# Windowed attention with sinks, then a gated MLP block: one load queue with casts on chip, transposes one phase earlier, gating bias on the tensor engine, a shared ring of four PSUM banks

## The chip, the cores and the metric

The kernel runs on one core of one Trainium2 chip. The metric is the device time of a whole execution in microseconds (us). Every kernel was run several times; "before" and the kernel compared with it ran on the same chip, in alternating rounds. Ratios use fast runs alone: a ratio is the mean time of one kernel's fast runs over that of the other's fast runs of the same rounds, so it isn't quite the ratio of the medians quoted beside it.

Names of engines in the profile: PE is the tensor engine (PEld its weight loads), DVE the vector engine, ACT the scalar engine, POOL the GpSimd engine, SP the engine that issues the loads and stores (SPq is its queue).

## The reference, cut to what matters

```python
# q, k, v: (4 batches, 8 heads, 768 positions, 64); n_sink = 4, window = 128
scores = (q @ k.T) / sqrt(64)
keep   = (pos_k < n_sink) | ((pos_q - pos_k >= 0) & (pos_q - pos_k < window))
x      = softmax(where(keep, scores, -1e9)) @ v          # -> (4, 768, 512)
h      = gelu_tanh(x @ w_in)                             # w_in: 512 x 1024
u, vv  = h[..., :512], h[..., 512:]
vn     = layer_norm(vv) * g_ln                           # over the 512 features
vs     = einsum('ts,bsd->btd', w_sg, vn) + b_sg[:, None] # mixes positions, 768 x 768
out    = x + (u * vs) @ w_out                            # f32, (4, 768, 512)
```

## The kernel before

Per batch the kernel has an attention part and an MLP part, and it weaves the attention of batch b+1 into the spatial mixing of batch b. The unit names below recur: T (cast and transpose q and k of a head pair), SK (scores against the sinks), QK, AV, XT (attention), MV (gate half of w_in, gelu, layer norm: the profile's hv, vt, z), MU (other half: hu, uT), SP (spatial mixing: vs, gatedT), OUT (ops, ot).

```python
ps_sc = tile_pool(name="ps_sc", bufs=2, space=PSUM)   # 2 tiles of 2 banks: sc, hv, hu
ps_av = tile_pool(name="ps_av", bufs=2, space=PSUM)   # attention results
ps_mm = tile_pool(name="ps_mm", bufs=2, space=PSUM)   # transposes, scs, vs, ops
...
def load_sinks(b):                                    # eight loads of 4 x 64 for each batch
    t = small.tile([n_sink * H, Dh], F32, name="vs32")
    for h in range(H):
        nc.sync.dma_start(out=t[n_sink * h:n_sink * (h + 1), :], in_=v[b, h, 0:n_sink, :])
...
def T(b, p):
    ...
    pcast(cb, src)                                    # q and k to bf16, both on POOL
    ps = ps_mm.tile([128, NT, 128], BF16, name="trp", tag="mm")
    for t in range(NT):
        nc.tensor.transpose(ps[:, t, :], cb[:, t, :, :], iden)
    # copy out of PSUM: q on DVE (qT), k on ACT (kT); then 2 small DVE copies into ks_sink
...
def QK(b, p, g):
    ...
    nc.scalar.activation(out=pt, in_=sc, func=Exp, scale=scale)
    nc.vector.tensor_mul(pt, pt, m)                   # band mask, every group on DVE
...
def MV(b, jj):
    ...
    nc.gpsimd.tensor_tensor(rs, rs, neg_half[:, 0:2], op=ALU.pow)
    for jl in range(2):                               # z = (vt - mean) * rs
        nc.vector.tensor_scalar(out=z[b][:, 2 * jj + jl, :], in0=vt[:, jl, :],
                                scalar1=mv[:, jl, 0:1], scalar2=rs[:, jl:jl + 1],
                                op0=ALU.subtract, op1=ALU.mult)
...
def SP(b, hf, dc):                                    # 6 products, then DVE, then POOL
    ...
    nc.vector.scalar_tensor_tensor(out=tmp, in0=ps[:, 0:NH], scalar=g_sb[:, dc:dc + 1],
                                   in1=b_bc[:, NH * hf:NH * (hf + 1)], op0=ALU.mult, op1=ALU.add)
    nc.gpsimd.tensor_mul(gatedT[b, hf][:, dc, :], tmp, uT[b][:, dc, NH * hf:NH * (hf + 1)])
...
# weights: three casting loads from the GpSimd queue, f32 in memory to bf16 on chip
nc.gpsimd.dma_start(out=w_in_sb, in_=moe_w_in.rearrange("(c p) f -> p c f", p=128))
...
for b in range(B):
    # MV and MU of batch b, with T(b+1, p) and load(b+2, p) between them;
    # then SP and OUT of batch b woven with SK, QK, AV, XT of batch b+1
```

The softmax here doesn't subtract the row's maximum and nothing guards it: scores larger than these inputs give would overflow.

## Time and profile before

The four runs of the kernel before had a median of 224.09 us (220.84 to 227.33). Two of them (224.35 and 227.33) lie over 1.5% above the fastest and count as slow. The profiled one took 222.34 us, of which 220.6 is the span.

I cut the span into stages. M of a batch starts at the first hv product that the others follow without a break; S starts at the first mixing product after the last z of the batch (a few products of rows already normalized come earlier). What stands ahead of M0 is the prologue: loads and the attention of batch 0.

| | prologue | M0 | S0 | M1 | S1 | M2 | S2 | M3 | S3 | tail |
|---|---|---|---|---|---|---|---|---|---|---|
| starts at, us | 0 | 36.5 | 68.3 | 95.1 | 116.2 | 142.9 | 160.7 | 187.1 | 201.5 | 217.3 |
| length, us | 36.5 | 31.8 | 26.8 | 21.1 | 26.7 | 17.8 | 26.4 | 14.4 | 15.8 | 3.3 |

Two windows of steady S stages are added here, for the comparison later. The columns are the stretch, its length, busy time of PE, PEld, DVE, ACT and POOL with the number of instructions, the granted PE clock, the DMA share and GB/s.

```profile
120.00:130.00 10.00, 7.75 (x93) 4.31 (x93) 9.08 (x15) 5.37 (x6) 4.49 (x4) 1.00 0.14 51
160.00:170.00 10.00, 8.02 (x69) 3.71 (x71) 7.72 (x12) 6.66 (x8) 4.77 (x4) 1.00 0.01 2
```

PE has gaps of some 2 us in 10, and DVE is the fuller engine in the first of the two.

### The profile page before, as it was taken

What the parts mean: (1) busy time and instruction counts of PE and PEld (TensorE: products, weight loads), DVE (VectorE), ACT (ScalarE), POOL (GpSimd) and SP (SyncE); (2) the same over time, 40 slices, a digit from 0 to 9 for tenths busy, and PEclk for the clock granted to TensorE, in tenths of its full rate; (3) what the DMA queues carried; (4) which work ended last, traced back from release to release, by engine and by line L of the source; (5) the groups of instructions that cost most, each with busy time, mean ns of one, the idle gap of its engine ahead of it and who ended that gap; (6) DMA issues with size and microseconds to landing.
All of it is one profiled execution on the core that took longest, in us unless ns stands there. A gap on an engine that the chain in (4) does not pass through costs nothing.

```text
span 220.6 us, 3819 instructions
## 1 busy us (share of the span) xinstructions
PE 165.1 (75%) x1444; PEld 92.8 (42%) x1460; DVE 152.3 (69%) x302; ACT 105.9 (48%) x123; POOL 97.2 (44%) x134
## 2 busy tenths in 40 slices
PE   0653767693959698699649599898796998798792
PEld 0331544351635465445424355545433555344340
DVE  3542788254897898737986898648968986276553
ACT  2250697532644455164758264375792643642000
POOL 8715822466662726506865506026144061034360
PEclk9999999889699999999999999999999999999999
DMA  6986999999994039299800040210000302100213
GB/s 197 266 155 185 279 230 221 306 287 314 289 312 115 0 113 248 54 269 250 211 8 0 0 146 1 95 51 0 0 3 0 143 3 95 48 4 0 76 68 143
DMA packets 39778, 28.59 MB, mean 130 GB/s; under 512 B 26576, under 2 KB 36048, under 8 KB 39760
## 3 DMA queue, kind: packets, MB, share of 16 engines
q1 hardware_dynamic: 37920, 25.60, 41.9%
q0 software_dynamic: 1840, 2.75, 6.9%
q8 instruction: 11, 0.18, 0.4%
q14 instruction: 7, 0.06, 0.1%
HBM read 24.81 MB, written 6.29 MB: 141 GB/s over the span
## 4 chain that ended last, share of the span: by engine, by line
DVE 33%; DMA 18%; PE 18%; POOL 11%; issue 7%; SPq 6%; ACT 4%; POOLq 1%; DVEq 0%; ACTq 0%
DVE z L271 8%; DVE pt L206 7%; PE ops L307 6%; POOL gatedT L301 6%; DMA v_104<-in_v_dram 6%; DMA b_bc<-in_moe_b_sg_dram 5%; DVE gtmp L298 4%; PE vs L294 4%; DVE st L265 3%; ACT pt L204 3%; DVE ot L310 3%; DVE qT L168 3%; POOL rs L269 3%; DMA v_544<-in_v_dram 3%; PE hv L254 3%
## 5 line engine op out<-in xcount | busy, mean ns | idle before, releaser
L301 POOL TENSOR_TENSOR gatedT<-gtmp,uT 128x384 bf16<-128x384 bf16 x32 | 33.9, 1066 | 50.9 <-DVE gtmp L298 50.5
L204 ACT ACTIVATE pt<-sc 128x1024 bf16<-128x1024 f32 (+1 forms) x48 | 43.9, 953 | 22.6 <-PE sc L199 22.4
L294 PE MATMUL vs<-wsgT,z 128*128 128x384 bf16 x192 | 36.6, 327 | 2.3 <-DVE z L271 1.1
L307 PE MATMUL ops<-w_out_sb,gatedT 128*128 128x512 bf16 x89 | 25.6, 381 | 12.0 <-POOL gatedT L301 10.6
L254 PE MATMUL hv<-w_in_sb,xT 128*128 128x512 bf16 x92 | 24.2, 397 | 3.8 <-ACT vt L260 2.1
L168 DVE COPY qT<-trp 128x768 bf16<-128x768 bf16 x16 | 15.2, 951 | 15.8 <-PE trp L164 15.7
L206 DVE TENSOR_TENSOR pt<-pt,mask_128 128x1024 bf16<-128x1024 bf16 (+1 forms) x32 | 25.0, 792 | 1.4 <-ACT pt L204 1.1
L244 ACT COPY xT<-xps 128x768 bf16<-128x768 bf16 x16 | 12.8, 803 | 26.1 <-PE xps L243 26.1
L281 PE MATMUL hu<-xT,w_in_sb 128*128 128x384 bf16 x128 | 24.5, 336 | 0.7 <-ACT uT L284 0.7
L298 DVE SCALAR_TENSOR_TENSOR gtmp<-vs,g_sb,b_bc 128x384 bf16<-128x384 f32 x32 | 19.5, 611 | 7.9 <-PE vs L294 7.9
L310 DVE TENSOR_TENSOR ot<-ops,x_sb 128x512 f32<-128x512 f32 x24 | 16.4, 690 | 11.2 <-PE ops L307 11.2
L294 PEld LDWEIGHTS <-z 128*128 128x128 bf16 x192 | 17.2, 97 | 16.4 <-issue 4.6
L271 DVE TENSOR_SCALAR z<-vt,mv,rs 128x512 bf16<-128x512 f32 x24 | 17.5, 768 | 8.2 <-POOL rs L269 8.2
L199 PE MATMUL sc<-qT,kT 64*128 64x256 bf16 x192 | 19.6, 280 | 2.3 <-DVE rcp L234 1.1
L219 PEld LDWEIGHTS <-pt 128*128 128x128 bf16 x192 | 15.0, 99 | 13.0 <-issue 6.5
L284 ACT ACTIVATE uT<-hu 128x768 bf16<-128x768 f32 x16 | 13.0, 814 | 12.4 <-PE hu L281 12.4
L265 DVE BATCH_NORM_STATS2 st<-vt 128x6 f32<-128x512 f32 x24 | 15.6, 673 | 4.2 <-ACT vt L260 4.2
L170 ACT COPY kT<-trp 128x768 bf16<-128x768 bf16 x16 | 12.8, 801 | 11.3 <-PE trp L164 11.3
L235 DVE TENSOR_TENSOR x_sb<-av,rcp 128x384 bf16<-128x384 f32 x32 | 17.5, 555 | 0.8
L307 PEld LDWEIGHTS <-gatedT 128*128 128x128 bf16 x96 | 8.3, 97 | 23.0 <-POOL gatedT L301 14.6
L164 PE MATMUL trp<-iden,qb 128*128 128x128 bf16 x96 | 9.5, 242 | 9.5 <-POOL qb L152 7.7
L281 PEld LDWEIGHTS <-w_in_sb 128*128 128x128 bf16 x128 | 12.5, 100 | 8.9 <-issue 2.0
(115 smaller groups left out, 262.4 us busy)
## 6 DMA issues: line engine op xcount, KB each, us to landing
out_dram<-ot SPq DMA_DIRECT2D x24, 256.0 KB
wsg_rows<-in_moe_w_sg_dram POOLq DMA_DIRECT2D x1, 1152.0 KB, 12.2
w_in_sb<-in_moe_w_in_dram POOLq DMA_DIRECT2D x1, 1024.0 KB, 12.3
w_out_sb<-in_moe_w_out_dram POOLq DMA_DIRECT2D x1, 512.0 KB, 10.1
q_94<-in_q_dram SPq DMA_DIRECT2D x1, 384.0 KB
k_96<-in_k_dram SPq DMA_DIRECT2D x1, 384.0 KB
v_98<-in_v_dram SPq DMA_DIRECT2D x1, 384.0 KB
q_100<-in_q_dram SPq DMA_DIRECT2D x1, 384.0 KB
```

The lines of the kernel that those rows point to most:

```text
L168: nc.vector.tensor_copy(dv, sv)
L204: nc.scalar.activation(out=pt[:, :, 0:w], in_=sc[:, :, 0:w], func=AF.Exp, scale=scale)
L206: nc.vector.tensor_mul(pt[:, :, 0:w], pt[:, :, 0:w], m.unsqueeze(1).to_broadcast([128, 2, w]))
L254: nc.tensor.matmul(hp[:, jl, :], xT[b][:, c, 128 * j:128 * (j + 1)], w_in_sb[:, c, d_half:2 * d_half], start=(c == 0), stop=(c == KD - 1))
L265: nc.vector.bn_stats(out=st, in_=vt[:, jl, :])
L271: nc.vector.tensor_scalar(out=z[b][:, 2 * jj + jl, :], in0=vt[:, jl, :], scalar1=mv[:, jl, 0:1], scalar2=rs[:, jl:jl + 1], op0=ALU.subtrac ...
L281: nc.tensor.matmul(hp[:, hf, 0:NH], w_in_sb[:, c, 128 * dc:128 * (dc + 1)], xT[b][:, c, NH * hf:NH * (hf + 1)], start=(c == 0), stop=(c == ...
L294: nc.tensor.matmul(ps[:, 0:NH], z[b][:, si, 128 * dc:128 * (dc + 1)], wsgT[:, si, NH * hf:NH * (hf + 1)], start=(si == 0), stop=(si == NT ...
L298: nc.vector.scalar_tensor_tensor(out=tmp, in0=ps[:, 0:NH], scalar=g_sb[:, dc:dc + 1], in1=b_bc[:, NH * hf:NH * (hf + 1)], op0=ALU.mult, op ...
L301: nc.gpsimd.tensor_mul(gatedT[b, hf][:, dc, :], tmp, uT[b][:, dc, NH * hf:NH * (hf + 1)])
L307: nc.tensor.matmul(ps, gatedT[b, hf][:, dc, 128 * tl:128 * (tl + 1)], w_out_sb[:, dc, :], start=(dc == 0), stop=(dc == KU - 1))
L310: nc.vector.tensor_add(ot, ps, x_sb[b][:, t, :])
```

## The change

The intent: take away what stands in the load queue at the start, take the transposes of the next batch out of M, shorten the way from mixing to output in S, and let PE run further ahead of the engines that empty its banks. The core of the diff, cut:

```diff
-    ps_av = ctx.enter_context(tc.tile_pool(name="ps_av", bufs=2, space=bass.MemoryType.PSUM))
-    ps_mm = ctx.enter_context(tc.tile_pool(name="ps_mm", bufs=2, space=bass.MemoryType.PSUM))
+    ps_mm = ctx.enter_context(tc.tile_pool(name="ps_mm", bufs=4, space=bass.MemoryType.PSUM))
+    wst = ctx.enter_context(tc.tile_pool(name="wst", bufs=2))       # f32 staging of weights
     # (stage 4 -> 3, ptile 6 -> 5, vpool 2 -> 3, opool 4 -> 3, zpool 3 new)
-    load_sinks(0)
+    nc.sync.dma_start(out=vs_all[:, 0:Dh], in_=v.rearrange("b h s d -> (b h) s d")[:, 0:n_sink, :])
+    load(0, 2)
 ...  T: casts of batch 0 go to DVE (q) and ACT (k); ks_sink built by one POOL multiply
 ...  QK, batches 1 to 3: the third group's mask
+            nc.gpsimd.affine_select(out=d0, in_=d0, compare_op=ALU.is_ge, fill=0.0, ...)
 ...  MV: z in two steps, half on ACT
+            if jl == 0:
+                nc.scalar.activation(out=zt, in_=vt[:, jl, :], func=AF.Identity,
+                                     scale=rs[:, jl:jl + 1], bias=nb[:, jl:jl + 1])
+            else:
+                nc.vector.tensor_scalar(out=zt, in0=vt[:, jl, :], scalar1=rs[:, jl:jl + 1],
+                                        scalar2=nb[:, jl:jl + 1], op0=ALU.mult, op1=ALU.add)
+            nc.vector.tensor_mul(z[b][:, 2 * jj + jl, :], zt, g_bc)
 ...  SP: bias as one more product, gating straight from PSUM on DVE
+        nc.tensor.matmul(ps[:, 0:NH], ones2, b_hl[:, NH * hf:NH * (hf + 1)], start=True, stop=False)
-        nc.vector.scalar_tensor_tensor(out=tmp, in0=ps[:, 0:NH], scalar=g_sb[:, dc:dc + 1], ...)
-        nc.gpsimd.tensor_mul(gatedT[b, hf][:, dc, :], tmp, uT[b][:, dc, NH * hf:NH * (hf + 1)])
+        nc.vector.tensor_mul(gatedT[b, hf][:, dc, :], ps[:, 0:NH], uT[b][:, dc, NH * hf:NH * (hf + 1)])
 ...  weights: plain f32 loads in the one SP queue, cast on chip
+    def load_w_in(c):
+        t = wst.tile([128, d_ff], F32, name="wst")
+        nc.sync.dma_start(out=t, in_=moe_w_in[128 * c:128 * (c + 1), :])
+        nc.scalar.copy(w_in_sb[:, c, :], t)
 ...  order: T(b+2, p) in the attention of batch b+1 (in S); T(1, p) still behind MU(0, p);
      output steps stand a few mixing steps behind their inputs
```

## The prediction

It was written with the profile of before alone.

> **What bounds the kernel now.** I read the page first, then the chain of waits, then the time line of single stretches. The page names no single bound:
>
> ```profile
> span 220.6 us, 3819 instructions
> ...
> PE 165.1 (75%) x1444; PEld 92.8 (42%) x1460; DVE 152.3 (69%) x302; ACT 105.9 (48%) x123; POOL 97.2 (44%) x134
> ...
> DVE 33%; DMA 18%; PE 18%; POOL 11%; issue 7%; SPq 6%; ACT 4%; POOLq 1%; DVEq 0%; ACTq 0%
> ```
>
> No engine is full over the span, and the chain changes hands, so I cut the span into stages by the first and last matmul of each kind (hv = gelu input of the gate half, scs/vs = start of spatial mixing and next attention). Reading the time line: loads and attention of batch 0 to 36.5 us; then per batch an M stage (both halves of w_in, gelu, layer norm, and the transposes of the next batch's q and k) and an S stage (spatial mixing, output, attention of the next batch). M0 36.5-68.3, S0 68.3-95.8, M1 95.8-116.2, S1 116.2-143, M2 143-160.8, S2 160.8-187.1, M3 187.1-201.1, S3 201.1-217.3, then the tail to 220.6.
>
> In the first stage the load queue is what to look at (time line, start us, length, what):
>
> ```profile
> 5.54 11.97 SPq L83 DMA_DIRECT2D vs_106<-in_v_dram  x8
> ...
> 17.55 0.40 SPq L71 DMA_DIRECT2D q_161<-in_q_dram  x1
> ...
> 19.00 1.03 POOL L146 TENSOR_TENSOR v_sink_143<-vs_106,headsel 32x512 bf16<-32x512 f32 x1 [7.38 <-DMA vs_106<-in_v_dram]
> ```
>
> Eight tiny sink loads hold the queue for 12 us; the third head pair's load is issued at 17.55 only, and PE waits 5.5 us for the sinks. In M0, POOL stands in order before loads:
>
> ```profile
> 48.00 0.83 POOL L152 TENSOR_SCALAR qb<-q_540 128x768 bf16<-128x768 f32 x1 [0.31 <-DMA q_540<-in_q_dram]
> 49.12 0.83 POOL L152 TENSOR_SCALAR kb<-k_542 128x768 bf16<-128x768 f32 x1 [0.29 <-DMA k_542<-in_k_dram]
> 50.67 0.84 POOL L152 TENSOR_SCALAR v_sb_146<-v_544 128x768 bf16<-128x768 f32 x1 [0.72 <-DMA v_544<-in_v_dram]
> 51.59 0.19 POOL L267 TENSOR_SCALAR rs<-mv 128x2 f32<-128x2 f32 x1
> ```
>
> The first layer-norm root (rs) has its input at 49.3 (the time line has the second mv at 49.13) but comes behind a cast whose load lands at 50.6; all of z, then the w_sg transposes at 60.8-67.3, follow late. In a steady S stage the costs are these groups:
>
> ```profile
> L301 POOL TENSOR_TENSOR gatedT<-gtmp,uT 128x384 bf16<-128x384 bf16 x32 | 33.9, 1066 | 50.9 <-DVE gtmp L298 50.5
> ...
> L307 PE MATMUL ops<-w_out_sb,gatedT 128*128 128x512 bf16 x89 | 25.6, 381 | 12.0 <-POOL gatedT L301 10.6
> ...
> L206 DVE TENSOR_TENSOR pt<-pt,mask_128 128x1024 bf16<-128x1024 bf16 (+1 forms) x32 | 25.0, 792 | 1.4 <-ACT pt L204 1.1
> ...
> L298 DVE SCALAR_TENSOR_TENSOR gtmp<-vs,g_sb,b_bc 128x384 bf16<-128x384 f32 x32 | 19.5, 611 | 7.9 <-PE vs L294 7.9
> ```
>
> DVE in one S stage: 8 gtmp x 0.61 + 12 masks x 0.79 + 6 ot x 0.69 + 8 x_sb x 0.555 + 8 rcp x 0.18 = 4.9+9.5+4.1+4.4+1.4 = 24.3 us of some 27. So S is bound by DVE, with waits of PE for POOL's gatedT on top.
>
> **What the Trainium skill says.** (1) SBUF — State Buffer, section Who interferes with whom: a DVE instruction with two SBUF inputs and a GpSimd one that reads SBUF lock each other out. The trace agrees: a 1024-wide mask takes 0.68 us at 117.91 and, two of them, 2.00 us from 119.32 beside POOL's multiplies. (2) VectorE: DVE Perf Modes, The perf-mode tier table: tensor_tensor with a PSUM operand runs at 1x. Agrees: x_sb from PSUM, 384 wide, 0.555 us; so replacing gtmp (0.608) by a PSUM multiply saves only some 0.05 each on DVE. (3) ScalarE: Activation LUTs, Table sets and What ACT_TABLE_LOAD costs: identity is filler in every set, and a load takes about 1283 ns. The trace has loads of 1283 ns, and copies after gelu without one; I count none for the new Identity. (4) DMA: Bandwidth & Descriptors, SWDGE vs HWDGE vs iDMA: a cast in a DMA is only possible from GpSimd. The software queue's 2.75 MB here is exactly the three weights in bf16; sent plain they are 5.5 MB, written bytes double.
>
> **The change part by part.**
>
> Loads. One sink load instead of 32; the queue no longer stands for 12 us. Batch 0 (4.72 MB) and w_in (2.10) arrive by some 6.8 MB / 0.275 = 25 us plus 2 to start; 275 GB/s is a little below what full stretches of before moved (277 in 20-30 us, 296-303 in 40-60). w_in has two staging buffers, each freed by an ACT cast (estimate 1.0 us, as a 1024-wide exp takes 1.02): chunk 3 can start only after chunk 1 is cast, so I add 3 us: M0 starts at about 30, not 36.5. Until the next batch's q/k/v are in, 15.2 MB must pass (4.72x2+2.10+2.36+1.05+0.3): 15.2/0.28 = 54 + 2, say 57 us. Before, the same data ended near 53, being 2.75 MB shorter. But M0's own work, some 15 us from 30 on, and the w_sg transposes no longer wait for it: POOL's roots come before the casts of batch 1. S0 starts near 60 (57 + cast 0.83 + six transposes 0.5 + copy 0.95 + the sink product): -8 us.
>
> M stages. For batches 1 to 3 the transposes leave M. M1 and M2 lose 4 x (0.95 qT copy on DVE, 8 small ks_sink copies x 0.23 per batch, 0.8 kT on ACT, 1.0 of PE). M3 of before has no transposes and took 14.0 us, so that is the first estimate. In M3 the third gelu waits until 195.82 for a vt buffer; with three it can run near 193.9, which brings the last z forward by about 2 us. Against it the new z: per batch 3 x (nb 0.2) + 3 Identity on ACT (estimate 0.6) + 3 on DVE (0.5 alone) + 6 bf16 multiplies by g (half of a 1024-wide mask, 0.35): DVE +0.6 +1.5 +2.1 against six z at 0.73 = 4.4, about equal. M = 12 each: M1 -8, M2 -6, M3 -2.
>
> S stages. DVE: gtmp becomes the gating multiply, 8 x -0.05 = -0.4; the third mask of each pair goes to POOL, 4 x -0.66 = -2.6; T comes in for S0 and S1: 4 x 0.95 = +3.8. So 24.3 becomes 25.1 in S0 and S1, and 21.3 in S2. PE gets 48 transposes (2.7 us at 0.055) and 8 bias products (8 x 0.16 = 1.3): from about 19.7 us of pure streaming (48 vs at 0.16, 24 ops at 0.215, transposes, attention) to 24. POOL: 8 x 1.07 goes, 12 casts x 0.83 + 12 selects (0.28 for 128 columns, estimate 0.45 for 256) + small = 17 us, not full. Removing the POOL hop takes about 1 us off each gate-to-output chain, and the output products are now a few mixing steps behind. S0 and S1: +1 each (28.5); S2: -2. S3 is near PE's streaming: 8 x 7 x 0.162 = 9.1 plus 24 x 0.215 = 5.2, 14.3 for 16.2: -2.
>
> Sum: -8 +1 -8 +1 -6 -2 -2 -2 = -26, so 195 us of span; the run times lie 1.7 over the span (222.34 against 220.6), and the median of the timed runs 2 above that one: 197 to 199. I take off a little of the gain for what a static in-order schedule usually leaves unfilled, and predict 200.
>
> **The rivals.** (a) The DMA takes over the start: more bytes, and two-deep staging with the whole load order in one queue. A load waiting for a buffer holds all behind it. For it: M0 already ran at 296-303 GB/s and the queue before shows standing loads. If staging costs 10 us, S0 starts near 70 and the time is about 209. (b) S stages become worse: PE, DVE and POOL all gain work there, and POOL's casts lock DVE's masks as gatedT did, while POOL's selects stand behind casts that wait for a load. At 32 us for S0 and S1 the time is 207. Against it, masks that can be hit are a third fewer. (c) M0 is hidden better than I think: if spatial mixing of batch 0 starts while batch 1 still lands (its z is ready near 45), S0's own work overlaps the loads, and the time falls to 192. (d) Nothing moves, the DMA-bound start hides all: contradicted by batches 2 and 3: in ten-microsecond windows from 140 us on the DMA moves 0 to 95 GB/s.
>
> **Range and chances.** (a) and (b) together give 214 at worst; (c) with the full sum 190. Eight in ten: 190 to 211. Within 2% means above 219.9, which needs all of (a), (b) and no gain in M1 and M2: 4%. Slower needs a new block that I don't see: 2%.
>
> **What would show it.** Right: no stretch of sink loads; load of the third pair issued before 8 us; first hv near 30; no cast between mv and rs in M0; M1 to M3 near 12 us each; S0 and S1 27-30 with DVE over 85% and no POOL between vs and ops. Wrong: a queue standing on a staging buffer in 10-55 us with DMA below 250 GB/s (a); POOL selects behind casts that wait for a load, or masks near 1.3 us (b); table loads other than two per batch (my third citation); M still near 18 us, then it wasn't the transposes.

## The result, and the profile after

The changed kernel took 204.62 us (median of 4 runs, 203.45 to 205.13), against 224.09: the ratio is 0.9196, with a 95% interval of 0.9069 to 0.9323. By the medians the gain is 19.5 us; by the fast runs alone it is 17.9. The profiled run took 204.31 us, its span is 202.4. A second set of runs gave 204.26 (experiment e5).

The page of the changed kernel, in the same lines as those that the prediction shows of before:

```profile
span 202.4 us, 3866 instructions
...
PE 166.9 (82%) x1476; PEld 96.3 (48%) x1492; DVE 140.0 (69%) x299; ACT 121.8 (60%) x143; POOL 77.1 (38%) x148
...
PE 42%; DVE 15%; POOL 13%; ACT 12%; DMA 8%; issue 5%; SPq 3%; POOLq 0%; ACTq 0%
```

DVE lost 12.3 us of work and POOL 20.1; ACT gained 15.9. The chain of waits has turned over: PE went from 18% to 42%, DVE from 33% to 15%, DMA from 18% to 8%. In the steady S stages of after (windows, columns as above) PE is nearly without a gap:

```profile
120.00:130.00 10.00, 9.91 (x126) 6.73 (x127) 8.37 (x18) 5.97 (x7) 2.50 (x7) 1.00 0.20 79
160.00:170.00 10.00, 9.89 (x125) 6.19 (x125) 8.59 (x20) 5.09 (x6) 2.31 (x6) 1.00 0.21 80
```

The groups of the S stage (line, engine, operation, names and shapes, count, busy us, mean ns, idle time ahead of them with its main releaser):

```profile
L344 PE MATMUL ops<-w_out_sb,gatedT 128*128 128x512 bf16 x86 | 24.0, 380 | 0.5
L338 DVE TENSOR_TENSOR gatedT<-vs,uT 128x384 bf16<-128x384 f32 x32 | 17.6, 553 | 8.7 <-PE vs L335 8.7
L233 POOL TENSOR_SCALAR_AFFINE_SELECT pt<-pt 128x256 bf16<-128x256 bf16 x24 | 9.7, 426 | 28.1 <-ACT pt L152 28.1
```

The output products waited 12.0 us in before, 10.6 of it for POOL; now 0.5. The gating multiply takes 0.553 us, as estimated (0.608 less 0.05), and the POOL select 0.43 (estimated 0.45).

At the start, the time line of the load queue (SPq) and of ACT:

```profile
5.23 3.26 SPq L84 DMA_DIRECT2D vs_all<-in_v_dram  x1
8.53 0.58 SPq L72 DMA_DIRECT2D q_111<-in_q_dram  x1
...
17.58 0.41 SPq L74 DMA_DIRECT2D k_587<-in_k_dram  x1
28.52 1.99 SPq L368 DMA_DIRECT2D wst<-in_moe_w_in_dram  x2
...
27.43 1.06 ACT L369 CAST w_in_sb<-wst 128x1024 bf16<-128x1024 f32 x1
```

The 12 us of sink loads are gone and the third pair's load goes out at 8.53 instead of 17.55. But after k_587 the queue stands from 17.99 to 28.52: the next load wants a weight staging buffer, and ACT, in its own order, gets to the first cast of w_in at 27.43 only. In the window of 20 to 30 us the DMA moves 136 GB/s, and ACT is busy 9.36 of 10:

```profile
20.00:30.00 10.00, 6.57 (x102) 4.86 (x100) 7.88 (x17) 9.36 (x12) 2.10 (x3) 1.00 0.39 136
```

The stages, side by side with the prediction's terms:

| | start (prologue + M0) | S0 | M1 | S1 | M2 | S2 | M3 | S3 | sum |
|---|---|---|---|---|---|---|---|---|---|
| before, us | 68.3 | 26.8 | 21.1 | 26.7 | 17.8 | 26.4 | 14.4 | 15.8 | |
| after, us | 65.4 | 27.9 | 15.3 | 26.2 | 14.1 | 22.9 | 14.4 | 13.2 | |
| difference | -2.9 | +1.1 | -5.8 | -0.5 | -3.7 | -3.5 | 0.0 | -2.6 | -17.9 |
| predicted | -8 | +1 | -8 | +1 | -6 | -2 | -2 | -2 | -26 |

(The tail after S3 is 3.3 us before and 3.0 after.) The range held and the kind of gain was right; the start fell short by 5 us, the M stages by 6.5 in all, and the S stages together gave 3.5 us more than predicted.

### The profile page after: what moved, and what is told of

Same layout as the page of the kernel before. It is cut to its first block, busy times and chain, and to the rows that moved or that the text cites. A ratio compares the mean times of both kernels' runs of the same rounds, so it can differ in the third digit from the quotient of the medians.

```text
span 202.4 us, 3866 instructions
## 1 busy us (share of the span) xinstructions
PE 166.9 (82%) x1476; PEld 96.3 (48%) x1492; DVE 140.0 (69%) x299; ACT 121.8 (60%) x143; POOL 77.1 (38%) x148
## 4 chain that ended last, share of the span: by engine, by line
PE 42%; DVE 15%; POOL 13%; ACT 12%; DMA 8%; issue 5%; SPq 3%; POOLq 0%; ACTq 0%
PE vs L335 10%; PE ops L344 9%; PE hv L286 5%; ACT pt L152 4%; POOL rs L301 4%; PE sc L220 3%; DMA vs_all<-in_v_dram 3%; DVE st L297 3%; DVE z L313 3%; DMA v_667<-in_v_dram 3%; PE trp L185 3%; PE av L251 3%; PE xps L275 2%; PE av L257 2%; DMA wst<-in_moe_g_ln_dram 2%
## 5 line engine op out<-in xcount | busy, mean ns | idle before, releaser
L335 PE MATMUL vs<-wsgT,z 128*128 128x384 bf16 x192 | 38.9, 327 | 4.5 <-DVE z L313 4.5
L152 ACT ACTIVATE pt<-sc 128x1024 bf16<-128x1024 f32 (+1 forms) x36 | 33.0, 960 | 8.7 <-PE sc L220 4.0
L335 PEld LDWEIGHTS <-z 128*128 128x128 bf16 x192 | 17.8, 98 | 19.3 <-DVE z L313 7.5
L286 PE MATMUL hv<-w_in_sb,xT 128*128 128x512 bf16 x91 | 22.5, 380 | 1.5 <-ACT xT L276 0.9
L338 DVE TENSOR_TENSOR gatedT<-vs,uT 128x384 bf16<-128x384 f32 x32 | 17.6, 553 | 8.7 <-PE vs L335 8.7
L321 PE MATMUL hu<-xT,w_in_sb 128*128 128x384 bf16 x128 | 22.4, 326 | 0.0
L297 DVE BATCH_NORM_STATS2 st<-vt 128x6 f32<-128x512 f32 x24 | 15.9, 678 | 9.0 <-ACT vt L152 8.5
L191 ACT COPY kT<-trp 128x768 bf16<-128x768 bf16 x16 | 12.8, 801 | 13.2 <-PE trp L185 13.2
L233 POOL TENSOR_SCALAR_AFFINE_SELECT pt<-pt 128x256 bf16<-128x256 bf16 x24 | 9.7, 426 | 28.1 <-ACT pt L152 28.1
L189 DVE COPY qT<-trp 128x768 bf16<-128x768 bf16 x16 | 15.2, 952 | 6.0 <-PE trp L185 5.9
L220 PEld LDWEIGHTS <-kT 64*128 64x128 bf16 x192 | 7.7, 97 | 20.2 <-issue 11.1
L152 ACT ACTIVATE vt<-hv 128x1024 f32<-128x1024 f32 x12 | 12.3, 1024 | 7.7 <-PE hv L286 7.5
L321 PEld LDWEIGHTS <-w_in_sb 128*128 128x128 bf16 x128 | 12.4, 98 | 8.4
L228 DVE TENSOR_TENSOR pt<-pt,mask_130 128x1024 bf16<-128x1024 bf16 (+1 forms) x20 | 14.5, 730 | 2.7 <-ACT pt L152 2.7
L228 DVE TENSOR_TENSOR pt<-pt,mask_122 128x1024 bf16<-128x1024 bf16 x16 | 12.6, 790 | 5.1 <-ACT pt L152 4.7
```

Source lines behind the costliest of these rows:

```text
L152: r = nc.scalar.activation(func=func, **kw)
L220: nc.tensor.matmul(sc[:, hl, 256 * jl:256 * jl + n], kT[b, p][rows, 128 * j:128 * (j + 1)], qT[b, p][rows, 128 * j:128 * j + n], start=Tru ...
L228: nc.vector.tensor_mul(pt[:, :, 0:w], pt[:, :, 0:w], m.unsqueeze(1).to_broadcast([128, 2, w]))
L286: nc.tensor.matmul(hp[:, jl, :], xT[b][:, c, 128 * j:128 * (j + 1)], w_in_sb[:, c, d_half:2 * d_half], start=(c == 0), stop=(c == KD - 1))
L297: nc.vector.bn_stats(out=st, in_=vt[:, jl, :])
L321: nc.tensor.matmul(hp[:, hf, 0:NH], w_in_sb[:, c, 128 * dc:128 * (dc + 1)], xT[b][:, c, NH * hf:NH * (hf + 1)], start=(c == 0), stop=(c == ...
```

## The experiments

Twelve kernels ran. To compare them I use one more cut that every kernel has: the time at which the last z of each batch is done. The four times and the end of the span divide it into five beats; the first is the start, the last is M3's rest with S3 and the tail.

| profile | beat 0 | beat 1 | beat 2 | beat 3 | last | span |
|---|---|---|---|---|---|---|
| before | 61.9 | 51.4 | 45.1 | 43.1 | 19.1 | 220.6 |
| after | 57.8 | 50.8 | 40.3 | 37.2 | 16.3 | 202.4 |
| e1, four weight staging buffers | 62.5 | 48.2 | 40.1 | 37.3 | 16.2 | 204.3 |
| e2, g folded away | 68.1 | 42.3 | 39.9 | 36.7 | 17.1 | 204.1 |
| e3, transposes back in M | 57.9 | 50.1 | 41.4 | 39.6 | 16.3 | 205.3 |
| e5, after itself | 56.5 | 50.7 | 39.9 | 37.2 | 16.3 | 200.6 |
| e6, w_in cast on POOL | 57.4 | 52.1 | 40.2 | 37.2 | 16.3 | 203.2 |
| e7, POOL hop back | 57.0 | 52.8 | 41.6 | 38.4 | 17.6 | 207.4 |
| e8, candidate 1 | 55.1 | 50.3 | 40.5 | 36.7 | 17.6 | 200.2 |
| e9, third mask back on DVE | 57.5 | 51.9 | 43.7 | 38.7 | 16.3 | 208.1 |
| e10, PSUM ring split again | 62.6 | 53.0 | 43.3 | 38.5 | 17.3 | 214.7 |
| e11, mixing first | 58.0 | 52.1 | 39.2 | 37.2 | 16.3 | 202.8 |
| e12, candidate 2 | 57.2 | 49.3 | 40.4 | 36.8 | 17.5 | 201.2 |

(e4 is left out: its profile is slow.) e1 to e4 ran as one set on one chip, e5 to e8 as a second, e9 to e12 as a third, each with seven runs of the kernel before (medians 222.37, 222.16, 221.85). e5 is the changed kernel again and serves as the control, though e1 to e4 and e9 to e12 ran on other chips. Differences in us are of the medians, slow runs included (one of four in e2, e5, e6 and e11, two in e4 and e12). By the fast runs alone (control 203.7) e10 is 12.6 us over the control, e9 6.2, e7 6.1 and e3 4.4.

One rival goes through the whole table: the granted clock of PE. The traces record it, and in beat 0 the kernels differ. PE had half its clock there for 5.6 us in after, 8.2 in e5, 9.5 in e1, 15.0 in e10 and 17.1 in e2. In beat 1 such stretches come to 0 to 7.6 us (4.7 in after, 5.4 in e5, 5.5 in e10, 7.6 in e1), and later to 3.4 at most for each beat. In these lines of the windows the clock is the third figure from the end (e2, then e10, then after):

```profile
40.00:50.00 10.00, 3.96 (x19) 1.83 (x17) 6.85 (x8) 2.08 (x2) 2.31 (x3) 0.50 0.64 188
...
30.00:40.00 10.00, 6.54 (x58) 4.11 (x60) 4.73 (x9) 7.33 (x10) 1.97 (x3) 0.53 0.75 203
...
30.00:40.00 10.00, 7.74 (x85) 4.85 (x86) 6.01 (x15) 7.83 (x11) 3.48 (x5) 0.83 0.75 212
```

If PE were the limit throughout, a stretch at half clock would cost half its length (an estimate, and the most that it can be). Whether the edits bring these stretches about is not shown. So for e1, e2 and e10 the later beats are firmer evidence than beat 0.

My theory after the result: (A) the missing 5 us at the start come from the standing queue, and (B) the S stages are now bound by PE, so what was freed on DVE isn't all paid out. The rivals come with each run.

### e5_control: the changed kernel itself

No edit.

> The changed kernel itself, as a control on the chip of this call: both theories 203 to 206, first mixing of batch 0 within 1 us of 65.4, stages within 0.5 us of those of its first profile.

Measured: 204.26 us (202.5 to 205.97), ratio to before 0.9205 [0.9123, 0.9288]. The spans of two profiles of the same kernel (202.4 and 200.6) differ by 1.8 us, 1.3 of it in beat 0. Differences of 1% between single profiles mean nothing here.

### e1_wst4: four staging buffers for the weights

```diff
-    wst = ctx.enter_context(tc.tile_pool(name="wst", bufs=2))
+    wst = ctx.enter_context(tc.tile_pool(name="wst", bufs=4))
```

(To make room, the two masks share one tile; same values.)

> The changed kernel with four weight staging buffers for two (the masks share one tile to make room); nothing else. Theory A (the load queue stood on a staging buffer from 17.6 to 28.5 us, and this is why the first stages gained 2.9 us where 8 were predicted): the second pair of w_in loads is issued before 20 us, the DMA moves over 250 GB/s in 20-30 us, spatial mixing of batch 0 starts near 60 for 65.4, time about 199-200. Rival B (loads are hidden by the in-order work of ACT, DVE and PE in the first batch): start of mixing stays within 1.5 us of 65.4, time 203-205.

Measured: 207.37 us (206.38 to 208.93), ratio 0.9449 [0.9358, 0.9541]: slower than the changed kernel. The load queue in the time line:

```profile
13.63 3.63 SPq L367 DMA_DIRECT2D wst<-in_moe_w_in_dram  x4
28.31 0.33 SPq L391 DMA_DIRECT2D wst<-in_moe_g_ln_dram  x1
...
31.88 11.64 SPq L372 DMA_DIRECT2D wst<-in_moe_w_sg_dram  x6
43.57 0.43 SPq L72 DMA_DIRECT2D q<-in_q_dram  x1
```

All four w_in loads go out in one piece at 13.63, as the theory wanted; then the queue stands until 28.31 all the same, now at the fifth use of a staging buffer. The buffers moved the wait and didn't take it away: what frees them is ACT, which still casts at 27 to 33 us. Worse, the attention of batch 1 begins later (its last sink score product at 70.06 instead of 66.05). Why is not shown. Six w_sg loads now run ahead of its second pair, but the k of its last pair lands earlier than in after (59.75 for 62.05, landing times of the traces); and PE's clock was at half from 56.4 to 70.0 us (55.7 to 62.5 in after). More buffers behind an engine that frees them in order is not a mend.

### e6_win_pool: w_in cast on POOL instead of ACT

```diff
-        nc.scalar.copy(w_in_sb[:, c, :], t)
+        nc.gpsimd.tensor_scalar(out=w_in_sb[:, c, :], in0=t, scalar1=1.0, scalar2=1.0,
+                                op0=ALU.mult, op1=ALU.mult)
```

> The changed kernel with the four casts of w_in on POOL for ACT; nothing else. Theory C (ACT, busy 24 of the 30 us from 10 to 40 us, sets the start: its casts come late in its order, so staging buffers stay full and the queue stands, and the last exps come late): the third w_in load is issued before 22 us for 28.5, first product of M0 at 31-33 for 35.4, first mixing of batch 0 at 60-63 for 65.4, time 1.5 to 2.5% under the control. Rival (the loads of batch 1 or the in-order work of DVE set the start of mixing): M0 starts earlier but mixing within 1 us of the control, time within 0.7%.

Measured: 205.09 us (203.17 to 207.47), ratio 0.9240 [0.9158, 0.9322], the same as the control. The third w_in load goes out at 25.28 (28.52 in after) and M0 begins at 33.1 (35.4 in after, 33.7 in the control), but mixing starts at 66.7 (65.4 in after, 64.1 in the control). The stand got 3 us shorter; the start didn't.

### e11_mix_first: mixing of batch 0 ahead of the last transposes of batch 1

In after, the first mixing product stands in PE's order behind all transposes of batch 1. Its own operands are ready earlier: the last z of batch 0 is done at 57.8. The last pair's data come late (k_683 lands at 62.05 by the trace, and POOL then casts it behind a cast of w_out):

```profile
57.61 0.46 SPq L74 DMA_DIRECT2D k_683<-in_k_dram  x1
58.12 0.46 SPq L76 DMA_DIRECT2D v_685<-in_v_dram  x1
...
63.48 0.83 POOL L168 TENSOR_SCALAR kb<-k_683 128x768 bf16<-128x768 f32 x1
...
66.05 0.39 PE L205 MATMUL scs<-qT,ks_sink_149 128*128 128x512 bf16 x1
```

```diff
-            if b == 0:
+            if b == 0 and d < 2:
                 T(1, d)
 ...
+        if b == 0:
+            for s in su[0:4]:              # four mixing units
+                s()
+            su = su[4:]
+            with tc.issue_after(last_vs["i"]):
+                T(1, 2)
+                T(1, 3)
```

> The changed kernel, but the first four mixing products of batch 0 come before the last two sets of transposes of batch 1 in PE's order (those wait for loads that land late). Theory (S0 starts late because PE's static order puts mixing behind transposes of batch 1, not because mixing's own operands are late: the last z is there at 57.8 us): first mixing product at 58 to 60 us instead of 64 to 65, time 199.5 to 202. Rival (the same transposes then stand in the middle of S0, and DVE and PE wait there instead; the loads set the end): first mixing product earlier all the same, but time 203.5 to 206.

Measured: 205.09 us (204.52 to 208.54), ratio 0.9242 [0.9154, 0.9330]. The two lines that decide, from its time line:

```profile
60.39 1.66 PE L336 MATMUL vs<-wsgT,z 128*128 128x384 bf16 x6
...
68.10 0.39 PE L205 MATMUL scs<-qT,ks_sink 128*128 128x512 bf16 x1
```

Mixing starts 5 us earlier (its first product with z at 60.4 for 65.6) and the time doesn't move: the rival holds. The last sink score product of batch 1 (scs, which wants the transposes of all its pairs) comes at 68.1, 2 us later than in after, and M1 begins at about 93 in both. S0 lasts until the attention of batch 1 is done, and that waits for the data and the transposes of its last pair; what mixing wins ahead of them isn't won at the end. Which of the two sets it stays open: in e8 the k of that pair lands at 58.5, 3.5 us earlier than in after, and the last sink score product comes at 65.4, only 0.6 earlier. With my own stage table I had been measuring the wrong mark: where S0 starts doesn't set when it ends.

### e4_before_sink1: the kernel before with one sink load for each batch

```diff
-        for h in range(H):
-            nc.sync.dma_start(out=t[n_sink * h:n_sink * (h + 1), :], in_=v[b, h, 0:n_sink, :])
+        nc.sync.dma_start(out=t, in_=v[b, :, 0:n_sink, :])
```

> The kernel before with its eight sink loads per batch made one. Theory A (as predicted: the queue's 12 us of small loads delayed the third head pair): that pair's load issued before 9 us for 17.55, first product of the M stage near 31 for 36.5, time 218-220. Rival B (the start of M0 is set elsewhere, by w_in or by the attention of the first batch, and M0 by the loads of batch 1): first product of M above 34, time within 2 us of the kernel before.

Measured: 227.28 us (224.0 to 228.31), ratio to before 1.025 [1.0061, 1.0439]: unclear at 2%, and certainly no gain, though only two of the four runs were fast. The profiled run was slow, so its durations prove nothing; its order shows that the third pair's load goes out at 7.71 instead of 17.55, as wanted. Why that brings nothing is only argued: in before the DMA engines weren't idle while the queue stood, since the casting w_in load came by the other queue (185 GB/s over the first 20 us), and with the pairs issued at once both share the engines. What the fast runs show is that to take the 12 us of sink loads out of the queue doesn't by itself shorten the kernel.

### e10_ring22: the PSUM ring split into two and two again

```diff
-    ps_mm = ctx.enter_context(tc.tile_pool(name="ps_mm", bufs=4, space=bass.MemoryType.PSUM))
+    ps_av = ctx.enter_context(tc.tile_pool(name="ps_av", bufs=2, space=bass.MemoryType.PSUM))
+    ps_mm = ctx.enter_context(tc.tile_pool(name="ps_mm", bufs=2, space=bass.MemoryType.PSUM))
 ...
-        av = ps_mm.tile([128, 3, 2, Dh + 1], F32, name="av", tag="mm")
+        av = ps_av.tile([128, 3, 2, Dh + 1], F32, name="av", tag="av")
```

> The changed kernel, but its ring of four PSUM banks, shared by mixing, output and attention results, is split again into two and two as in the kernel before (attention results have two of their own). Theory (the shared ring is what lets PE run ahead of the DVE that drains it in S): S stages 1 to 2 us longer each, time 207 to 212. Rival (two buffers each were enough once POOL's hop is gone; the ring is worth nothing): within 1% of the changed kernel, 203 to 206.

Measured: 216.54 us (215.12 to 216.81), ratio 0.9746 [0.9681, 0.9811]: 12.3 us slower than the control, more than the theory's 7.7 at most, and far from the rival. The table of beats shows it everywhere: +4.8, +2.2, +3.0, +1.3, +1.0 against after. The waits of PE (who waited for whom: us in total, times, longest) name a mechanism:

```profile
PE trp L186 <- DVE wsgT L381: 1.7, 1, 1.7
...
PE trp L186 <- DVE qT L190: 1.3, 2, 0.8
PE vs L334 <- DVE gatedT L339: 1.0, 3, 0.3
...
PE trp L186 <- DVE ot L348: 0.8, 2, 0.6
PE trp L186 <- DVE gatedT L339: 0.7, 1, 0.7
```

A transpose doesn't read wsgT, ot or gatedT. These are waits for a bank: the transposes share two banks with mixing and output and must wait until DVE has emptied one. None of these five stands in the list of after; together they are 5.5 us. This is the largest single part that I measured. By stages S0 is 30.5 us (27.9 in after) and S1 30.3 (26.2). Two reservations. The static order of the instructions may have changed with the ring, and the 12.3 us are those of the ring together with the order it allows. And in beat 0 PE was at half clock 9.4 us longer than in after, which can make up to 4.7 of the 4.8 us there; the 7.5 us of the later beats fall at much the same clock as in after. Whether the transposes could stand in S only with a shared ring is not shown: no kernel here has the split ring with the transposes in M.

### e3_t_in_m: transposes of batches 2 and 3 back in M

```diff
-            if b == 0:
-                T(1, d)
+            if nxt:
+                T(b + 1, d)
 ...
-                au.append(lambda p=p: (load(b + 2, p), T(b + 2, p)))
+                au.append(lambda p=p: load(b + 2, p))
```

(The staging of q and k got four buffers, so that the loads don't wait for M.)

> The changed kernel with the transposes of batches 2 and 3 back in the M stage of the batch before them (their loads still issued in the stage before; four buffers for q and k so that they can be held). Theory A (moving them was worth several us because M has idle engines only in name): M1 and M2 back to 19 and 17 us, S0 and S1 shorter by 1 to 2, time 209-211. Rival B (the work only changes place): M1 and M2 up by 3, S0 and S1 down by 3, time 203-206.

Measured: 207.37 us (207.29 to 210.26), ratio 0.9458 [0.9346, 0.9569]: 3.1 us over the control by the medians, 2.7% by the ratios, which are of two sets; between the two expectations. By stages against after, with the marks of the stage table: S0 23.2 (-4.7), M1 20.6 (+5.3), S1 23.1 (-3.1), M2 18.7 (+4.6), S2 23.7 (+0.8). The transposes cost nearly as much where they went as they had cost where they came from. (M1 and M2 of e3 each hold 3.4 us at half clock, those of after none; up to 1.7 us of each may be that.) The prediction's estimate of what they add to S0 and S1 (4 qT copies at 0.95, 3.8 us) is about what the two show, 3.9 on average.

### e7_pool_hop: the POOL step between mixing and output put back

```diff
-        nc.vector.tensor_mul(gatedT[b, hf][:, dc, :], ps[:, 0:NH], uT[b][:, dc, ...])
+        tmp = gpool.tile([128, NH], BF16, name="gtmp")
+        nc.vector.tensor_scalar(out=tmp, in0=ps[:, 0:NH], scalar1=1.0, scalar2=1.0, ...)
+        nc.gpsimd.tensor_mul(gatedT[b, hf][:, dc, :], tmp, uT[b][:, dc, ...])
```

The bias stays on PE and the order of the units stays; the DVE step itself takes the same time (0.557 us for 0.553).

> The changed kernel with the gate as before in its path: DVE writes a bf16 copy of the PSUM result, POOL multiplies by u. Bias product and order of the output units stay. Theory A (the POOL hop in the path was worth the 3.3 us by which the last stage shrank): S3 15-16.5 us for 12.9, S0 to S2 each longer by 0.5 to 1.5, time 206-210. Rival B (the new order of output units hides the hop; S3 shrank through the order): S3 within 1 us of 12.9, time within 1% of the control.

Measured: 209.75 us (209.07 to 210.71), ratio 0.9494 [0.9431, 0.9557]: 5.5 us over the control. Its waits of PE have a line that the control doesn't have:

```profile
PE ops L346 <- POOL gatedT L340: 3.3, 5, 1.5
```

All beats from the second on are longer: +2.1, +1.7, +1.2, +1.3 against the control. So this is the worth of the POOL step, and it falls in every S stage. It isn't the wait alone: beside POOL's multiplies the 1024-wide masks on DVE take 0.887 us each for 0.795 in the control, 2.8 us over the 32 of them, and how the 5.5 us divide is not shown. The prediction had it inside its -2 for S2 and S3.

### e9_mask_dve: the third mask of each pair back on DVE

```diff
-        if g < NG - 1 or b == 0:
+        if True:
```

> The changed kernel, but the third causal mask of each head pair is multiplied on DVE again for batches 1 to 3 (256 wide at bf16, as before), instead of selected on POOL. The prediction counted this move as 4 x 0.66 = 2.6 us of DVE in each of three S stages. Theory (the S stages of the changed kernel are bound by PE, which is 9.8 to 9.9 of 10 busy there against 8.4 to 8.6 on DVE): under 1 us for each S stage, time 204 to 207, within 1.5% of the changed kernel. Rival (the S stages are still bound by DVE, as the prediction took them): +2 to +2.6 us for each of S0, S1 and S2, time 210 to 213.

Measured: 209.77 us (209.06 to 211.06), ratio 0.9461 [0.9396, 0.9526]: 5.5 us over the control. The theory (PE-bound, at most 207) failed; the rival's 210 to 213 was just missed. The page:

```profile
PE 169.6 (82%) x1476; PEld 97.0 (47%) x1492; DVE 145.7 (70%) x311; ACT 121.7 (58%) x143; POOL 64.0 (31%) x112
```

DVE has 12 instructions and 5.7 us more than in after, and the span is 5.7 us longer. PE has the same 1476 products and is "busy" 2.7 us longer. Against the control the beats grow by 1.0, 1.2, 3.8, 1.5 and 0: a part of the masks falls into M. (In one stretch of this profile, 110 to 136 us, the granted clock was 0.93, so a little of beat 2 may be that.) So a stage where PE is busy 9.9 of 10 is not bound by PE alone. Why the 9.9 misleads can be read off the groups: a mixing product is recorded with 327 ns, but six in a row take 1.14 us, that is 0.16 apiece and 0.16 at the end. Each record carries a tail of that size, and a gap no longer than the tail doesn't show. The Trainium skill, page Perfetto Trace Analysis, section Identifying the Most-Contended Engine, says that the busy share of matmuls is no good measure of how near a kernel is to its limit, and names the share of peak arithmetic and the busy share of the weight loads instead. PEld is busy 6.2 to 6.7 of 10 in those windows, which leaves room, and putting work back on DVE cost its full time.

### e2_g_fold: no multiply by g in M

```diff
-            zt = zpool.tile([128, d_half], BF16, name="zt")
+            zt = z[b][:, 2 * jj + jl, :]
-            nc.vector.tensor_mul(z[b][:, 2 * jj + jl, :], zt, g_bc)
 ...  w_out's rows are multiplied by g in their cast; the bias product has 1/g on its other side
+        nc.vector.reciprocal(t[0:3, 0:d_half], t[0:3, 0:d_half])
```

> The changed kernel without the six multiplications by g per batch: g goes into the rows of w_out when they are cast, and the bias product gets b/g. Same result within tolerance. Theory A (the new layer norm's g multiply and the longer chain behind the last gelu ate the M stage's gain, 14.1-15.3 us where 12 was predicted): M1, M2, M3 each shorter by 1.5 to 2.5 us, time about 198-199. Rival B (M is bound by PE and ACT): M stages within 0.5 us of 15.3, 14.1, 14.4, time 203-205.

Measured: 206.85 us (205.72 to 209.04), ratio 0.9385 [0.9297, 0.9473]: slower than the control by 2.6 us by the medians, with an interval that clears the control's by 0.001 only. The loss is in the start (beat 0 is 68.1 for 57.8, beat 1 gives 8.5 of it back). One line of DVE's time line:

```profile
39.36 3.33 DVE L398 RECIPROCAL wst<-wst 3x512 f32<-3x512 f32 x1
```

A reciprocal on three rows of 512 took 3.33 us, in DVE's order ahead of the last attention results of batch 0, and PE stands from 41.2 to 46.4 for these. That isn't all of it: PE's clock was at half from 36.0 to 53.0 us (in after from 31.8 to 35.2), and how the loss divides is not shown. In e8, with the reciprocal early, it doesn't appear (beat 0 is 55.1). M1, M2 and M3 are shorter by 0.6, 0.6 and 1.6 us than in after, where I had expected 1.5 to 2.5 each. But from the first hv to the last z all three are as expected, 13.7, 12.4 and 12.6 us for 15.3, 14.1 and 14.3; in M1 and M2 mixing then begins only 1.1 us after the last z (0.06 in after). Of M3's 1.6 little is left at the end: from the first hv of batch 3 to the end it is 29.7 us for 30.6. In after, PE had used the wait for z to do mixing products of the positions already normalized (12 before the last z, for 7 in e2); with z earlier the other five come after it.

### e8_best1 and e12_best2: two candidates

e8 puts together: w_in cast on POOL, the value sinks of batches 1 to 3 built after the first roots, g folded away with its reciprocal early, where DVE is idle. e12 is e8 with the order of e11.

> The version that the findings point to: w_in cast on POOL, the value sinks of batches 1 to 3 made after the layer norm's roots instead of in the first stage, and g folded into w_out and the bias product with its reciprocal taken in DVE's idle time at the start. Theory C with the folded g's measured -0.6, -0.6 and -1.6 us in M1 to M3: first mixing at 59-62, time 195-199. Rival (static order gives back what is taken out): not under 202.

> The best candidate: POOL casts w_in, the value sinks of the later head pairs are built after the first roots, the scale of the layer norm is folded into w_out, with its reciprocal early, and the first four mixing products of batch 0 come before the last transposes of batch 1. Theory (start set by orders on ACT, POOL and PE, each taken away here): time 197 to 200. Rival (the arrival of the loads sets the start of batch 1's attention, whatever the orders): 202 or more, as the same kernel without the reordering of mixing had 202.3.

Measured: e8 202.31 us (200.57 to 202.91), ratio 0.9131 [0.9061, 0.9200]; e12 203.7 us (200.68 to 205.19), ratio 0.9098 [0.8990, 0.9206], from only two fast runs of four. The control has 0.9205 [0.9123, 0.9288]. Both miss their expectations of 195 to 200; the intervals overlap with the control's, so neither is shown to be better than the changed kernel. In both the last sink score product of batch 1 comes at 65 to 66 us, as in after; over the seven profiles where I looked for it (after, e1, e5, e6, e8, e11, e12) it lies at 64.7 to 70.1 us and never earlier.

## Why the prediction was right or wrong, point by point

**The reading of before** held: the sink loads, the cast between a load and the roots, and POOL between mixing and output were real. The first and the last are gone from the path; a cast still stands ahead of the first root (see the marks below).

**The start, -8, was mis-sized; it measured -2.9.** The failing step is "chunk 3 can start only after chunk 1 is cast, so I add 3 us". ACT's cast takes 1.06 us, as estimated, but it doesn't begin when the chunk lands; it begins at 27.43, behind the attention work in ACT's order. The queue stands for 10.5 us. In numbers: the prediction let 15.2 MB pass by 57 us at 280 GB/s; the trace shows a mean of 241 GB/s over the first 58 us, which is 14.0 MB, and the missing 1.2 MB is 4.3 us at 280. (The 280 came from full stretches; over the same 58 us before had moved 246.) The window of 20 to 30 us alone (136 GB/s for the 277 of before) lost 1.4 MB. That is rival (a), at half the size given there. e4 shows that the sink loads weren't the start's bound by themselves, e11 that mixing's place in PE's order isn't, e1 that more buffers aren't the mend. That the standing queue is the cause fits e1 and e6, but isn't shown: no kernel here took the stand away whole, and the best had 200 GB/s in that window. What the start would be without it stays open. It isn't the only stand either: in after the queue stands again from 53.79 to 57.19, for the last w_out load needs the buffer of the last w_sg rows, which landed at 54.85; DVE casts them at 56.61 only, behind a layer norm step that waits for POOL's root. PE waits 3.8 us for the same cast, and the k of batch 1's last pair leaves at 57.61, behind this stand. No experiment took it away alone.

**M1 -8 and M2 -6 were put too high; they measured -5.8 and -3.7, and M3 0.0 for -2.** That the transposes leave M was right: put back, they cost 5.3 and 4.6 us there (e3). The failing step is "M = 12 each", by way of "about equal" for the new z. From the first hv to the last z, before had 18.2, 15.5 and 14.4 us and after has 15.3, 14.1 and 14.3; the rest of the gain (2.9 and 2.3 us in M1 and M2) lies between the last z and the first mixing product, where the last copies of the transposes and the sink scores had stood. The sub-step on the third vt buffer was right. In before (time line), gelu of the third group comes 8.7 us after the stage's start and the last z is done 4.6 us after gelu's end:

```profile
195.82 1.02 ACT L260 ACTIVATE vt<-hv 128x1024 f32<-128x1024 f32 x1
...
200.48 1.00 DVE L271 TENSOR_SCALAR z<-vt,mv,rs 128x512 bf16<-128x512 f32 x2 [1.09 <-POOL rs L269]
```

In after it comes at 6.2 us, 2.5 earlier, but what follows is longer:

```profile
178.05 1.02 ACT L152 ACTIVATE vt<-hv 128x1024 f32<-128x1024 f32 x1 [1.35 <-PE hv L286]
...
180.88 1.08 DVE L313 TENSOR_TENSOR z<-zt,g_bc 128x512 bf16<-128x512 bf16 x3
181.88 0.54 DVE L311 TENSOR_SCALAR zt<-vt,rs,nb 128x512 bf16<-128x512 f32 x1
182.43 0.66 DVE L297 BATCH_NORM_STATS2 st<-vt 128x6 f32<-128x512 f32 x1
...
184.85 0.81 ACT L308 ACTIVATE zt<-vt,nb,rs 128x512 bf16<-128x512 f32 x1 [0.52 <-DVE nb L303]
185.37 0.76 DVE L313 TENSOR_TENSOR z<-zt,g_bc 128x512 bf16<-128x512 bf16 x2
```

From the end of gelu to the end of the last z it is 7.1 us for 4.6. The sum of DVE times was about right, but DVE's order has the second group's steps ahead of the third group's statistics (it stands 0.86 us for POOL's root before the first of these, and does three multiplies by g and one zt, 1.5 us, before the second), and the Identity on ACT takes 0.81 us, not 0.6. A sum of durations was used for what is a chain. That the multiply by g is a part of it is shown by e2 (1.6 to 1.7 us to the last z in each of the three); the rest was only read from the trace.

**S0 and S1, +1 each, measured +1.1 and -0.5: right.** Inside, the estimate of 3.8 us for the transposes is near what e3 shows (4.7 in S0, 3.1 in S1); the masks' -2.6 for each stage came out as 5.5 us in all (e9) for 7.8.

**S2 -2 and S3 -2 measured -3.5 and -2.6.** The mis-sized term is the POOL hop, taken as about 1 us on a chain and worth 5.5 us over the kernel (e7, with what it does to the masks).

**What the prediction left out: the ring.** The title names it and the working gives it no term, yet it is the part whose absence costs most (12.3 us, e10). That S0 and S1 came out right was luck in this respect: with two and two banks they took 30.5 and 30.3 us (e10). That is most of the way to rival (b)'s 32, with waits for banks in the list, and not by POOL's casts or locked masks as written there.

The single parts put back cost 12.3, 5.5, 5.5 and 3.1 us (e10, e7, e9, e3), 26.4 in all and more than the whole gain of 19.5 by the same medians. They are not additive: each was removed from a kernel in which the others rely on it.

**The marks** that the prediction named: third pair's load before 8 us (8.53, nearly); first hv near 30 (35.4, wrong); no cast between mv and rs in M0 (wrong: mv at 44.99, a cast at 45.21, rs at 46.12; it costs some 0.9 us where before lost over 2); two table loads for each batch (eight, right); no POOL between vs and ops (right); M1 to M3 near 12 us each (15.3, 14.1 and 14.4, wrong); S0 and S1 at 27 to 30 with DVE over 85% (27.9 and 26.2, with 8.5 of 10 from 80 to 90 us and 8.4 from 120 to 130: nearly). Of the signs of being wrong, (a)'s came, a queue standing on a staging buffer with 136 GB/s; (b)'s masks near 1.3 us didn't (0.78 on average, 1024 wide).

**A slip in the sums.** (a) at 209 and (b) at 207 are 9 and 7 us over the predicted 200, so together 216, not 214.

## What to carry to other kernels

Before moving work into a stage, count where its results land: the PSUM banks that it shares with what is there already may be worth more than the work itself. Don't price a chain by the sum of its durations, and don't take a busy tensor engine for the bound: put work back on its neighbour and see whether the time grows. A load queue whose staging buffers are freed by an engine with its own long order stands when that engine is late; ask for each buffer when it is freed, not how long the freeing takes.

## What the Trainium skill lacked or had wrong

- Perfetto Trace Analysis, section Matmuls, advises to rotate independent groups through PSUM banks so that evacuation and matmuls overlap. It is right, but gives no size and doesn't say whether banks are better shared or split by purpose. Here a shared ring of four against two and two is worth 12.3 us of 216.5, 7.5 of them in beats where the granted clock was much the same.
- None of the pages that I looked up gives the time of a reciprocal on DVE by its length: 3x512 took 3.33 us, where 128x6 takes 0.18 to 0.20.
